# Linear attention with RMS norm and an ELU layer: the first group as four single-head-pair chains in single-bank tiles, three product buffers in the first two groups, and one norm moved behind its group's products

## The chip, the core and the metric

The kernel runs on one core of a Trainium2 chip. The core has TensorE (PE: matmuls, and PEld for its weight loads), VectorE (DVE), ScalarE (ACT), GpSimd (POOL) and SyncE (SP), each with its own instruction queue worked in order, and DMA queues that move data between the chip's memory and the core's on-chip memory SBUF. Matmul results land in PSUM, which has eight banks; one bank holds 512 fp32 columns on 128 partitions, and a tile of 1024 columns takes two. The metric is device time in microseconds. The span of a profile is counted from the first to the last instruction.

## The reference

For 8 batches and 8 heads, with 576 rows and a head dimension of 64:

```python
kv = einsum('bhsd,bhse->bhde', k, v)
out = einsum('bhsd,bhde->bhse', q, kv)
rms = sqrt(mean(out * out, axis=-1, keepdims=True) + 1e-06)
x = (out / rms * g_norm)           # then (b, s, h*d): 4608 tokens of 512
h = x @ w_in                       # 512 x 2048
g = where(h > 0, h, exp(minimum(h, 0)) - 1)
return g @ w_out                   # 2048 x 512
```

Inputs and outputs are fp32; the kernel multiplies in bf16 and sums in fp32.

## The kernel before

The 4608 tokens are worked in nine groups `T` of 512: groups 0 to 7 are the first 512 rows of each batch, group 8 is the last 64 rows of all eight. A group passes through these steps:

- **Attention.** `kv_single` multiplies k by v per head (72 small matmuls for a batch, `at["kv"]`, or two halves `kv0` and `kv1`). `se_mm` multiplies the transposed q by it, in two halves of 256 tokens (`se0`, `se1`). ACT squares (L223), DVE sums per head (L228, `sum`), ACT takes logarithm and exponential for the inverse root (L234 and L235, `inv`), DVE scales (L238, `mul`). The result is turned so that features lie on partitions, by TensorE (`x0`, `x1`, L299, emptied by ACT or DVE at L306 and L308) in groups 1 and 2, or by a transposing DMA on SP (`xd`, then `xg` on DVE) later. q is turned by TensorE in groups 0 and 1, and by a transposing DMA (`qd`, L260) after.
- **First layer.** `mm1(T, i)` for `i` of 0 to 7 makes 256 of the 2048 columns of `h`: two accumulations of four 512-column matmuls (L382), in a PSUM tile of two banks. `elu` follows: ACT takes Exp (L394); then a min and a subtraction (L403) on `eng`, which is VectorE or, in two products of group 0, GpSimd; then DVE takes the max with `h` out of PSUM (L411). With `relu`, ACT also takes a Relu of `h` (L398) and DVE adds instead, from SBUF.
- **Second layer.** `mm2(T, j, f0, f1)` sums 128 tokens `j` over 16 blocks `f` of 128 columns (L427). `mm2_quarter` does four blocks. ACT copies the result (L437) and SP stores two `j` at a time.

Nothing reorders the work: a manual schedule is set, so each engine runs its instructions in the order in which the code issues them. The framework adds semaphores where a tile is read after it is written, and where a buffer is used again.

PSUM is shared out at the start into three pools: `ps_at` (one tile of two banks, for attention), `ps_m1` (two tiles of two banks, for first-layer products) and `ps_m2` (two tiles of one bank, for second-layer sums). With `spare=True`, `mm1` puts its product into the two `ps_m2` banks.

**Group 0** has its own attention code (L495 to L614), in which features lie on partitions from the start. q comes as fp32 in two halves `s`, is cast by DVE and ACT, and turned. Then come two rounds `u`, each with two head pairs `c`: `kv_first`, `se_first`, `square_first`, `mean_first` (a matmul with a matrix of 1/64), `log_first`, `exp_first`, `scale_first`. In round 0 the two `se0` share one tile of two banks, and so do the two `mean0`. Matmuls of zeros (`idle`) stand between the steps; their results are not used. After that come sixteen first-layer matmuls (L621), by blocks `c` of features, then `mm1(0, 2)` to `mm1(0, 7)`, with the ELU step of products 3 and 5 on GpSimd, and q of batch 1 turned after product 5.

**Group 1's attention** is issued between the quarters of group 0's second layer (L649 to L671). The last quarters of `j` 2 and 3 stand after `mm1(1, 0)`, those of `j` 0 and 1 inside group 1's loop. **`group`** (L690) issues the eight products with the next group's attention (`start` gives the product after which each step stands) and with pieces of the group before's second layer (`second`). In group 1, `se0` of group 2 comes after product 5 and `se1` after product 7, both in the attention tile; the sums, the inverse root and the scaling follow one product later, and `mm2(1, 0)` and `mm2(1, 1)` stand at its end with the turnings.

POOL issues the loads of k, v, w_in, w_out and the later q, in the order of the code, between its own computing; each load waits for the landing of the eighth before it. SP loads batch 0's q and issues the stores and the transposing DMAs.

Of the kernel before, what the change touches and what calls it, by code (L numbers as in the profile page):

```python
# [16 lines left out]
def kernel(  # L17
# [36 lines left out]
    ps_at = ctx.enter_context(tc.tile_pool(name="ps_at", bufs=1, space=bass.MemoryType.PSUM))  # L54
    ps_m1 = ctx.enter_context(tc.tile_pool(name="ps_m1", bufs=2, space=bass.MemoryType.PSUM))
    ps_m2 = ctx.enter_context(tc.tile_pool(name="ps_m2", bufs=2, space=bass.MemoryType.PSUM))
# [110 lines left out]
    def kv_single(T, kv_ps, u):  # L167

        for j in range(RK):
            for l in range(2):  # L170
                for s in range(2):
                    rows = slice(s * 64, s * 64 + 64)
                    nc.tensor.matmul(  # L173
                        kv_ps[l * 64 : l * 64 + 64, s, u * 64 : u * 64 + 64],
                        lhsT=bf["k", T][rows, j, 2 * u + l, :],
                        rhs=bf["v", T][rows, j, 2 * u + l, :],
                        start=(j == 0),
                        stop=(j == RK - 1),
                    )
# [65 lines left out]
    def attention(T):  # L245
        st = {}

        def q_t():
# [5 lines left out]
            nc.scalar.copy(qT[:, 0:2, :], qt_ps[:, 0:2, :])  # L254
# [111 lines left out]
    def mm1(T, i, cols=(slice(0, 512),), relu=False, spare=False, eng=nc.vector):  # L366
# [22 lines left out]
        return elu(T, i, parts, relu, eng)  # L389

    def elu(T, i, parts, relu, eng):
# [9 lines left out]
        def rest():  # L401
            for lo, hi, h in parts:
                eng.tensor_scalar(  # L403
# [60 lines left out]
    for u in range(2):  # L464
        fetch_packed_kv("k", 0, slice(2 * u, 2 * u + 2))
        if u == 1:
            make_identity(nc, ident)
        fetch_packed_kv("v", 0, slice(2 * u, 2 * u + 2))
# [14 lines left out]
    for s in range(2):  # L483
# [11 lines left out]
    q_st = q_tile(0)  # L495
    qt_ps = [
        ps_m2.tile([P, DM], FP32, name="qt_ps", tag="mm2").bitcast(BF16).rearrange(
            "p (r t) -> p r t", r=2
        )
        for _ in range(2)  # L500
    ]
# [5 lines left out]
    idle_a = ps_m1.tile([P, 2, G], FP32, name="idle_ps", tag="mm1")  # L507
    idle(idle_a[:, 0, :], 9)
    qT0 = attp.tile([P, NPAIR, G], BF16, name="qT", tag="qT")
    for s in range(2):  # L510
        for eng, js in ((V, slice(0, 2)), (A, slice(2, 4))):
            copy_on(eng, bf["q", 0][:, js, 4 * s : 4 * s + 4, :], q_st[:, js, 4 * s : 4 * s + 4, :])
        for p in range(2):
            q_t_mm(bf["q", 0][:, :, 4 * s : 4 * s + 4, :], qt_ps[s], p)
        if s == 0:
            nc.vector.tensor_copy(out=qT0[:, 0:2, :], in_=qt_ps[0])
            idle(idle_a[:, 0, :], 2)
    nc.scalar.copy(qT0[:, 2:4, :], qt_ps[1])
    nc.tensor.matmul(
        idle_a[:, 1, 0:1],  # L520
# [5 lines left out]
    nc.vector.tensor_copy(out=g_col, in_=idle_a[:, 1, 0:1])  # L526
    idle(idle_a[:, 0, :], 6)

    kv_ps = at_tile(FP32).rearrange("p (s x) -> p s x", s=2)
# [5 lines left out]
    se0, mean0 = {}, {}  # L535

    def kv_first(u):
        kv_single(0, kv_ps, u)
        nc.vector.tensor_copy(out=kv0[:, u], in_=kv_ps[:, :, u * 64 : u * 64 + 64])

    def se_first(u):
        for l in range(2):
            ls = slice(l * 64, l * 64 + 64)
            for s in range(2):
                nc.tensor.matmul(
                    se0[2 * u + l][s * 64 : s * 64 + 64, :],
                    lhsT=kv0[ls, u, s, :],
                    rhs=qT0[ls, 2 * s + u, :],
                    start=True,
                    stop=True,  # L550
                )
# [22 lines left out]
    mean_a = ps_m1.tile([P, 2, G], FP32, name="mean_ps", tag="mm1")  # L574
    se_a = ps_m1.tile([P, 2, G], FP32, name="se_ps", tag="mm1")
    idle_b = ps_m2.tile([P, DM], FP32, name="idle_ps", tag="mm2")
    for c in range(2):
        se0[c], mean0[c] = se_a[:, c, :], mean_a[:, c, :]
    kv_first(0)
    idle(idle_b, 1)  # L580
    se_first(0)
    square_first(0, A)
    square_first(1, V)
    idle(idle_b, 3)
    mean_first(0)
    idle(idle_b, 1)
    mean_first(1)
    log_first(0)
    exp_first(0)
    log_first(1)  # L590
    kv_first(1)
    idle(idle_b, 1)
    for c in range(2, 4):
        se0[c] = ps_m2.tile([P, DM], FP32, name="se_ps", tag="mm2")
    se_first(1)
    scale_first(0)
    square_first(2, A)
    exp_first(1)
    square_first(3, V)
    scale_first(1)  # L600
    firsts = [ps_m1.tile([P, 2, G], FP32, name="h_ps", tag="mm1") for _ in range(2)]
    mean_b = at_tile(FP32).rearrange("p (c f) -> p c f", c=2)
    for c in range(2, 4):
        mean0[c] = mean_b[:, c - 2, :]
    idle(firsts[0][:, 0, :], 3)
    mean_first(2)
    log_first(2)
    exp_first(2)
    idle(firsts[0][:, 0, :], 1)
# [4 lines left out]
    scale_first(3)  # L614

    gT[0] = mlpg.tile([P, FC, G], BF16, name="gT", tag="gT")
    firsts = [ps_m1.tile([P, 2, G], FP32, name="h_ps", tag="mm1") for _ in range(2)]
    for cs in ((0, 1), (2,), (3,)):
        for f in range(4):
            for c in cs:  # L620
                nc.tensor.matmul(  # L621
                    firsts[f // 2][:, f % 2, :],
                    lhsT=w_in_sb[:, c, f * P : f * P + P],
                    rhs=x0[:, c, :],
                    start=(c == 0),
                    stop=(c == KC - 1),
                )
# [154 lines left out]
```

## Time and profile before

| | us |
|---|---|
| median of 7 runs | 301.32 (300.65 to 302.5) |
| the profiled execution | 301.71, span 299.8 |
| TensorE busy | 281.8 (94% of the span) |
| VectorE busy | 169.0 (56%) |
| ScalarE busy | 142.4 (47%) |
| GpSimd busy | 57.2 (19%) |
| granted TensorE clock, mean | 0.994 |

The stages, from the start of the span, by the timeline:

| us | stage |
|---|---|
| 1.2 to 9.9 | first loads, q of batch 0 cast and turned |
| 9.9 to 20.2 | attention of group 0 |
| 17.8 to 35.4 | first layer of group 0 |
| 35.4 to 54.4 | second layer of group 0, attention of group 1 |
| 54.4 to 84.0 | rest of group 1, attention of group 2 |
| 84.0 to 107.4 | group 2, attention of group 3 |
| 107.4 to 299.8 | groups 3 to 8 and the last store |

An average of 94% over such stages says little about any one of them. A stretch in which TensorE is full gives nothing back to a change elsewhere. In a stretch with holes, what counts is which engine's wait ends last. A row of the timeline gives the start, the length, the engine and line, what it writes and reads, and in brackets how long the engine stood idle before it and what ended that.

### The profile page before, as it was taken

The numbers are of one execution on the slowest core, as the hardware profiler recorded it, in microseconds if no ns is written. First come the engines' busy times: TensorE is split into PE (matmuls) and PEld (weight loads), VectorE is DVE, ScalarE is ACT, GpSimd is POOL, SyncE is SP. The second block draws the span as 40 slices with busy tenths as digits, with TensorE's granted clock in tenths as the row PEclk, the third lists the DMA queues.
The fourth block names the chain that finished last, engine by engine and source line by source line (L and its number), as shares of the span: only waits on it lengthen the run. The fifth ranks groups of instructions, "written<-read, shape, count | busy, mean of one in ns | idle before, by whom it ended". The sixth has DMA issues, their size and how long they took to land.

```text
span 299.8 us, 4843 instructions
## 1 busy us (share of the span) xinstructions
PE 281.8 (94%) x2017; PEld 134.7 (45%) x2017; DVE 169.0 (56%) x210; ACT 142.4 (47%) x200; POOL 57.2 (19%) x81
## 2 busy tenths in 40 slices
PE   7888789886988999999999999999999999999995
PEld 2334345443444444444444444444444444444444
DVE  5264753468238875774676467646754776544400
ACT  3378643677236545534553455444543553433311
POOL 8434925161065006000400000001100000000000
PEclk9999999999899999999999999999999999999999
DMA  8999999999999959945931505163515031101132
GB/s 197 206 205 204 140 175 193 131 220 129 187 207 170 122 132 171 176 46 129 165 110 35 128 14 108 35 149 89 149 37 140 0 108 35 70 2 70 56 84 72
DMA packets 55898, 35.97 MB, mean 120 GB/s; under 512 B 32708, under 2 KB 53444, under 8 KB 55876
## 3 DMA queue, kind: packets, MB, share of 16 engines
q0 software_dynamic: 20128, 17.30, 39.0%
q1 hardware_dynamic: 35348, 17.83, 28.5%
q10 hardware_dynamic: 400, 0.52, 0.5%
q8 instruction: 16, 0.26, 0.3%
q14 instruction: 6, 0.05, 0.0%
HBM read 36.70 MB, written 9.44 MB: 154 GB/s over the span
## 4 chain that ended last, share of the span: by engine, by line
PE 82%; ACT 5%; DVE 5%; DMA 5%; POOL 1%; issue 1%; SPq 0%; DVEq 0%; ACTq 0%; POOLq 0%
PE h_ps L382 35%; PE o_ps L427 34%; PE o_ps L741 5%; DMA qT<-q_bf 5%; ACT elu_e L394 3%; PE at L204 2%; DVE gT L411 2%; PE idle_ps L505 2%; PE at L173 1%; POOL elu_e L403 1%; PE h_ps L621 1%; DVE xs L238 1%; ACT r L564 1%; ACT elu_h L398 1%; PE at L299 1%
## 5 line engine op out<-in xcount | busy, mean ns | idle before, releaser
L382 PE MATMUL h_ps<-xT,w_in_sb 128*128 128x512 bf16 (+1 forms) x568 | 131.6, 376 | 4.4 <-DVE gT L411 3.5
L427 PE MATMUL o_ps<-w_out_sb,gT 128*128 128x512 bf16 x512 | 122.8, 383 | 0.8 <-ACT o_sb L437 0.8
L394 ACT ACTIVATE elu_e<-h_ps 128x1024 bf16<-128x1024 f32 (+1 forms) x74 | 73.8, 1003 | 92.8 <-PE h_ps L382 91.2
L411 DVE TENSOR_TENSOR gT<-elu_e,h_ps 128x1024 bf16<-128x1024 bf16 (+1 forms) x65 | 78.3, 1204 | 11.7 <-POOL elu_e L403 5.3
L382 PEld LDWEIGHTS <-w_in_sb 128*128 128x128 bf16 x568 | 54.3, 98 | 66.2 <-issue 5.4
L427 PEld LDWEIGHTS <-gT 128*128 128x128 bf16 x512 | 50.3, 99 | 61.3 <-issue 3.4
L403 DVE TENSOR_SCALAR elu_e<-elu_e 128x1024 bf16<-128x1024 bf16 x70 | 31.4, 448 | 72.1 <-ACT elu_e L394 72.0
L437 ACT COPY o_sb<-o_ps 128x512 f32<-128x512 f32 x32 | 18.8, 586 | 22.6 <-PE o_ps L427 22.6
L228 DVE TENSOR_REDUCE ss<-sq 128x16 f32<-128x1024 bf16 x16 | 19.4, 1218 | 9.7 <-ACT sq L223 9.6
L147 POOL COPY q_bf<-q_pk 128x512 bf16<-128x512 bf16 x24 | 14.7, 657 | 36.8 <-DMA q_pk<-in_q_dram 17.6
L238 DVE TENSOR_TENSOR xs<-at,ss 128x1024 bf16<-128x1024 f32 x15 | 18.3, 1217 | 0.6 <-ACT ss L235 0.6
L223 ACT ACTIVATE sq<-at 128x1024 bf16<-128x1024 f32 x15 | 15.4, 1027 | 3.3 <-PE at L204 3.3
L121 POOL DMA_DIRECT2D k_pk<-in_k_dram x10 | 7.6, 756 | 43.5 <-PE at L173 40.2
L147 POOL CAST q_bf<-st_q 128x512 bf16<-128x512 f32 x4 | 2.6, 652 | 66.2 <-DMA st_q<-in_q_dram 66.2
L741 PE MATMUL o_ps<-w_out_sb,gT 128*128 128x512 bf16 (+1 forms) x80 | 14.0, 337 | 0.0
L204 PE MATMUL at<-bd_kv,qT 128*128 128x128 bf16 x104 | 7.9, 219 | 4.5 <-DVE xs L238 3.2
L204 PEld LDWEIGHTS <-qT 128*128 128x128 bf16 x112 | 7.2, 98 | 8.2 <-issue 4.4
L741 PEld LDWEIGHTS <-gT 128*128 128x128 bf16 x80 | 7.8, 98 | 6.2
L107 POOL DMA_DIRECT2D q_pk<-in_q_dram x14 | 10.4, 752 | 0.5 <-DMA v_pk<-in_v_dram 0.5
L345 ACT CAST bd_kv<-at 64x256 bf16<-64x256 f32 x14 | 5.1, 366 | 9.7 <-PE at L173 9.6
L505 PE MATMUL idle_ps<-zeros 128*128 128x512 bf16 x23 | 8.1, 479 | 1.5 <-DVE zeros L480 1.2
L403 POOL TENSOR_SCALAR elu_e<-elu_e 128x512 bf16<-128x512 bf16 (+1 forms) x3 | 7.5, 2500 | 4.9 <-ACT elu_e L394 4.8
(64 smaller groups left out, 111.7 us busy)
## 6 DMA issues: line engine op xcount, KB each, us to landing
out_dram<-o_sb SPq DMA_DIRECT2D x16, 512.0 KB, 3.2
q_pk<-in_q_dram POOLq DMA_DIRECT2D x14, 256.0 KB, 7.6
k_pk<-in_k_dram POOLq DMA_DIRECT2D x6, 576.0 KB, 10.6
v_pk<-in_v_dram POOLq DMA_DIRECT2D x6, 576.0 KB, 12.8
w_in_sb<-in_moe_w_in_dram POOLq DMA_DIRECT2D x4, 512.0 KB, 12.6
w_out_sb<-in_moe_w_out_dram POOLq DMA_DIRECT2D x4, 512.0 KB, 7.5
k_pk<-in_k_dram POOLq DMA_DIRECT2D x4, 288.0 KB, 11.3
v_pk<-in_v_dram POOLq DMA_DIRECT2D x4, 288.0 KB, 10.4
```

Of the source, the lines that this page charges most:

```text
L147: eng.tensor_copy(out=out_, in_=in_)
L204: nc.tensor.matmul(ov[:, u, :, s, :], lhsT=qT(p, j), rhs=bd_kv[:, T, p, :], start=True, stop=True,)
L223: nc.scalar.activation(sq, se_ps, AF.Square)
L228: nc.vector.reduce_sum(out=ss, in_=sq.rearrange("p c (h e) -> p (c h) e", h=H), axis=AX.X)
L238: nc.vector.tensor_tensor(out=xs.rearrange("p c (h e) -> p (c h) e", h=H), in0=se_ps.rearrange("p c (h e) -> p (c h) e", h=H), in1=ss.to_b ...
L382: nc.tensor.matmul(h_ps[a][:, cs], lhsT=w_in_sb[:, c, f * P : f * P + P], rhs=x(c, cs), start=(c == 0), stop=(c == KC - 1),)
L394: nc.scalar.activation(e[:, lo:hi, :], ps, AF.Exp)
L403: eng.tensor_scalar(out=e[:, lo:hi, :], in0=e[:, lo:hi, :], scalar1=1.0, scalar2=1.0, op0=ALU.min, op1=ALU.subtract,)
L411: nc.vector.tensor_tensor(out=gT[T][:, 2 * i + lo : 2 * i + hi, :], in0=e[:, lo:hi, :], in1=h, op=ALU.add if relu else ALU.max,)
L427: nc.tensor.matmul(o_ps[T, j], lhsT=gT[T][:, f, j * P : j * P + P], rhs=w_out_sb[:, f, :], start=(f == 0), stop=(f == FC - 1),)
L437: nc.scalar.copy(o_sb[T][:, j % 2, :], o_ps.pop((T, j)))
L741: nc.tensor.matmul(ps, lhsT=gT[B][:, f, j * P : j * P + P], rhs=w_out_sb[:, f, cols], start=(f == 0), stop=(f == FC - 1),)
```

## The change

- k and v of batch 0 are loaded head pair by head pair, in eight transfers.
- Group 0's attention uses a pool `ps_head` of its own, over all eight banks: two for kv, six single ones. The three later pools are opened when it closes, with `reuse_waits="tile"`, so that a tile waits for the readers of the banks that it takes over.
- The rounds become four steps `c`, one head pair each. The casts and copies of q are shared out otherwise between DVE and ACT, and there are 23 idle matmuls where there were 27.
- The first two products of group 0 lie in a `ps_m1` tile and in the attention tile. Products 3 and 6 of group 0, and 2 and 5 of group 1, go into the `ps_m2` banks. All ELU steps are on VectorE. Relu is used in products 0, 4 and 7 of group 0 and 1 and 4 of group 1.
- One of the two copies of group 1's transposed q goes from ACT to DVE.
- All quarters of group 0's second layer are done before group 1's first product, in the order of `j` 2, 3, 0, 1. That product is no longer cut into column halves.
- Group 1 is written out: `se0` of group 2 after product 6, `se1` after all products and half of `mm2(1, 0)`, in a `ps_m1` tile of its own; then the sums and scalings, 24 second-layer matmuls, and the turnings with a quarter of `mm2(1, 2)` after each. The rest of `mm2(1, 2)` and `mm2(1, 3)` stands beside products 1 to 6 of group 2.

```diff
-    def kv_single(T, kv_ps, u):
+    def kv_single(T, kv_ps, u, ls=(0, 1)):
...
-            for l in range(2):
+            for l in ls:
...
-            nc.scalar.copy(qT[:, 0:2, :], qt_ps[:, 0:2, :])
+            nc.vector.tensor_copy(out=qT[:, 0:2, :], in_=qt_ps[:, 0:2, :])
             nc.scalar.copy(qT[:, 2:4, :], qt_ps[:, 2:4, :])
...
-    for u in range(2):
-        fetch_packed_kv("k", 0, slice(2 * u, 2 * u + 2))
-        if u == 1:
+    for c in range(4):
+        fetch_packed_kv("k", 0, slice(c, c + 1))
+        if c == 2:
             make_identity(nc, ident)
-        fetch_packed_kv("v", 0, slice(2 * u, 2 * u + 2))
+        fetch_packed_kv("v", 0, slice(c, c + 1))
...
+    kv_ps = ps_head.tile([P, 2, G], FP32, name="kv_ps", tag="kv")
+    se0 = {c: bank(c) for c in range(2)}
+    idle_ps, g_ps = bank(2), bank(3)
...
-    for s in range(2):
-        for eng, js in ((V, slice(0, 2)), (A, slice(2, 4))):
...
+    for s, eng in ((0, A), (1, V)):
+        for js in (slice(0, 2), slice(2, 4)):
+            copy_on(
+                V if (s, js.start) == (0, 0) else eng,
...
+        copy_on(eng, qT0[:, 2 * s : 2 * s + 2, :], qt_ps[s])
         if s == 0:
...
-    idle(idle_a[:, 0, :], 6)
+    idle(idle_ps, 1)
...
+    kv_first(0)
+    idle(idle_ps, 1)
+    se_first(0)
+    square_first(0, A)
...
+    for c in range(2):
+        mean0[c] = bank(2 + c)
+    kv_first(1)
+    mean_first(0)
+    log_first(0)
+    idle(idle_ps, 1)
+    se_first(1)
+    square_first(1, A)
+    exp_first(0)
+    idle(idle_ps, 2)
+    kv_first(2)
+    mean_first(1)
+    log_first(1)
+    scale_first(0)
...
+    head.close()
+    ps_at = ctx.enter_context(tc.tile_pool(name="ps_at", bufs=1, space=bass.MemoryType.PSUM, reuse_waits="tile"))
...
-    elu(0, 0, [(0, 2, firsts[0])], True, V)()
-    elu(0, 1, [(0, 2, firsts[1])], False, V)()
+    for i in range(2):
+        elu(0, i, [(0, 2, firsts[i])], i == 0)()
     for i in range(2, 8):
-        mm1(0, i, relu=i in (2, 4, 6), spare=i in (2, 5), eng=Q if i in (3, 5) else V)()
+        mm1(0, i, relu=i in (4, 7), spare=i in (3, 6))()
...
-    for j in range(J):
+    order = (2, 3, 0, 1)
+    for j in order:
         mm2_quarter(0, j, 0)
...
-    rest = mm1(1, 0, (slice(0, 256), slice(256, 512)))
-    for j in (2, 3):
+    for j in order:
         mm2_quarter(0, j, 3)
-    rest()
...
-    second = {2: [(0, 0, 12, 16)], 3: [(0, 1, 12, 16)]}
-    group(1, at, {"kv": 2, "se0": 5, "se1": 7}, second, (1, 3, 5, 7), 1)
+    for i in range(8):
+        rest = mm1(1, i, relu=i in (1, 4), spare=i in (2, 5))
+        rest()
+        if i == 3:
+            at["kv"]()
+        if i == 6:
+            at["se0"]()
+    mm2(1, 0, 0, 8)
+    at["se1"](ps_m1.tile([P, 2, G], FP32, name="se_ps", tag="mm1"))
+    for n in range(2):
+        at[f"sum{n}"]()
+        at[f"inv{n}"]()
+    at["mul0"]()
+    at["mul1"]()
+    mm2(1, 0, 8, FC)
+    mm2(1, 1, 0, FC)
+    at["x0"]()
+    mm2_quarter(1, 2, 0)
+    at["x1"]()
+    mm2_quarter(1, 2, 1)
...
-            second = {i: [(1, 2 + i // 4, 4 * (i % 4), 4 * (i % 4) + 4)] for i in range(8)}
+            quarters = [(1, 2 + i // 4, 4 * (i % 4), 4 * (i % 4) + 4) for i in range(2, 8)]
+            second = {i + 1: [piece] for i, piece in enumerate(quarters)}
```

## The prediction

> **What bounds it now.** I read the page's shares first, then the table of stretches, the list of TensorE's waits, and last the timeline of the first 110 us. In the shares PE leads; the stretches (length, then busy time of each engine, granted clock, DMA share, GB/s) say where it is not full:
>
> ```profile
> PE 281.8 (94%) x2017; PEld 134.7 (45%) x2017; DVE 169.0 (56%) x210; ACT 142.4 (47%) x200; POOL 57.2 (19%) x81
> ```
> ```profile
> 110.00:280.00 170.00, 169.52 (x1131) 79.50 (x1130) 105.27 (x124) 77.60 (x108) 11.74 (x18) 1.00 0.44 90
> ...
> 70.00:74.00 4.00, 1.69 (x15) 0.93 (x13) 3.76 (x5) 2.80 (x5) 0.00 (x0) 1.00 1.48 117
> 74.00:78.00 4.00, 4.00 (x13) 1.50 (x11) 2.49 (x3) 1.16 (x3) 0.00 (x0) 0.57 1.47 122
> ```
>
> From 110 to 280 us PE is full (169.5 of 170) and the change leaves that code alone, so all that can move lies before group 3's first product at 107.43. At 70 to 74 us PE works 1.69 of 4 us, and then it runs at a clock of 0.57. TensorE's waits in that first part (total, times, longest):
>
> ```profile
> PE h_ps L382 <- DVE gT L411: 3.5, 4, 1.6
> PE at L204 <- DVE xs L238: 3.2, 2, 2.3
> ```
>
> A product waits until VectorE has emptied a PSUM buffer, and group 2's second attention product until the first one's scaling is done. The timeline (start, length, what, idle before) dates them:
>
> ```profile
> 13.34 0.38 PE L561 MATMUL mean_ps<-sq,means 128*128 128x512 bf16 x1 [0.86 <-DVE sq L558]
> 13.76 0.69 ACT L564 ACTIVATE r<-mean_ps,eps_col 128x512 f32<-128x512 f32 x1 [1.91 <-PE mean_ps L561]
> 19.41 0.75 DVE L570 SCALAR_TENSOR_TENSOR xT<-se_ps,g_col,r 128x512 bf16<-128x512 f32 x1 [0.49 <-ACT r L567]
> 20.96 1.02 ACT L394 ACTIVATE elu_e<-h_ps 128x1024 bf16<-128x1024 f32 x1 [1.59 <-PE h_ps L621]
> ...
> 26.89 3.64 POOL L403 TENSOR_SCALAR elu_e<-elu_e 128x1024 bf16<-128x1024 bf16 x1 [4.82 <-ACT elu_e L394]
> 31.84 3.61 PE L382 MATMUL h_ps<-xT,w_in_sb 128*128 128x512 bf16 x16 [1.55 <-DVE gT L411]
> ...
> 72.97 0.61 PE L204 MATMUL at<-bd_kv,qT 128*128 128x128 bf16 x8 [2.31 <-DVE xs L238]
> 73.42 5.30 PE L427 MATMUL o_ps<-w_out_sb,gT 128*128 128x512 bf16 x16
> 83.98 1.89 PE L382 MATMUL h_ps<-xT,w_in_sb 128*128 128x512 bf16 x8 [0.91 <-DVE xT L308]
> ```
>
> The first mean is done at 12.27, but its logarithm starts at 13.76, after the second mean: both lie in one tile. POOL's ELU step takes 3.64 us, and PE stands 1.55 behind it. The sixteen matmuls at 73.42 take 5.30 us; the next sixteen, at 79.00, take 3.62: the slow clock costs 1.7.
>
> **The sum, stage by stage.** I follow each engine in program order, with these durations: eight 512-column matmuls 1.73; ACT Exp or Relu over 1024 columns 1.02, the next starting 0.92 after it, over 512 0.55; DVE min 0.43, max out of PSUM 1.22 (512 columns: 0.69), add after a Relu 0.69; square 0.60; log then exponential 0.71; kv copy 0.29; scaling 0.75. Between engines: kv copy to product 0.05, product to square 0.46, mean to log 0.42, last scaling to ELU 0.80. All are read off the timeline.
>
> *Head.* DVE casts q's second half twice (6.10 to 7.1) and copies its transpose (7.65 to 8.34) where ACT did; ACT takes the first half's copy (1.01 against DVE's 0.69, still done at 7.14). Idle matmuls here go from six to one, and they no longer wait for g. So the first kv product moves from 9.89 to 8.3, its copy (behind g's on DVE) to 8.75, the first square from 11.24 to 9.55. Then, pair by pair: mean 10.2, log 10.62; second square 11.2; exponential 11.75; second mean 11.85; third product 12.5, square 12.96; fourth product 13.55; DVE copies and squares it 14.0 to 15.4; fourth mean 15.46, log 15.88, exponential 16.59, scaling 17.26 to 18.0; ELU 18.8 against 20.96: **2.15 us gained**. That the pools close behind this costs nothing: in the built order each new tile waits for the last reader of its own banks, the latest being the second scaling (16.1), and the third and fourth have other banks.
>
> The loads: batch 0's k and v become eight transfers of 144 KB instead of four of 288. That is four more issues of 0.75 on POOL, and w_in is issued from 7.8 instead of 4.79, each part also behind one of the first four pieces (landed by about 9). The queue is still fed, as k and v end only at 11.9, so I cost it at nothing; without that cover, each us it stands dry delays all later weights by one.
>
> *Group 0.* DVE gets three ELU steps back from POOL (7.5 us there, 3 x 0.43 here), one Relu fewer (+0.53 on DVE, -0.92 on ACT), and half of the qT copy (0.69). Against that PE has a third place for products (in 3 and 6 of 0 to 7, and the first pair uses the attention tile). Products 2 to 4 run unbroken from 19.05 to 24.25; product 5 waits for DVE's third max, 25.07 (0.85 lost); transposes 26.85 to 27.93; 6 and 7 to 31.4. The two halves of the qT copy are now in line: ACT's waits for DVE's, which stands behind the fifth max (29.8), so it runs 30.5 to 31.55 and delays Exp 6 behind it. Only k.v of batch 1 (31.55) and two quarter products (max 6 done at 34.0) meet that, and the order 2, 3, 0, 1 puts others before them. Second kv half 35.45; attention products 36.8 (40.69 before, the same 1.35 after); first turning 42.85; the last four quarters 45.65 to 50.1, with the same wait for the o_sb copy inside (0.8). Before, an equal amount of work was done at 54.45: **4.35 gained so far**.
>
> *Group 1.* PE's work from there is 25.7 us: eight products 13.84, kv 0.78, two attention products 1.22, 40 second-layer matmuls 8.63, two turnings 1.22. Each product finds its place empty: product 3 needs max 0 by 55.3, done 54.8; 5 needs max 2 by 59.55, done 58.35; 6 needs max 3 by 61.3, done 60.1. The second attention product has a tile of its own and needs max 6 (66.1) at 67.1, not the first one's scaling: the 2.31 goes. What is late next is DVE: max 7, two sums and two scalings in a row, 67.2 to 73.0, beside 24 matmuls; the first turning (72.9) finds its scaling done (71.85). Only four matmuls now part the turnings, so the second waits for ACT to empty the first (74.85): 0.55 lost. Group 2 begins at 76.45. Before it began at 83.98 with 1.73 less done, so 85.7: **9.25 gained so far**.
>
> *Group 2.* Its first and last products have no second-layer piece beside them, and DVE needs 1.65 a product and 2.44 a norm half. The second attention product still waits for the scaling (88.05; 0.7 against 0.86), and group 3's first product, with 2.6 us behind product 6's matmuls, waits for its max and the last g scaling (99.05; 0.85 against 0.34). Group 3 starts at 99.05 against 107.43. **Sum: -8.4 us.** The profiled execution took 301.71 (span 299.8 and 1.9 around it), so 293.3; it lies 0.4 over the median of the seven.
>
> **Loads now come near.** They run at about 190 to 205 GB/s written, and land (POOL waits for them):
>
> ```profile
> 10.47 0.70 POOL L121 DMA_DIRECT2D k_pk<-in_k_dram  x1 [0.70 <-DMA k_pk<-in_k_dram]
> 11.89 0.71 POOL L121 DMA_DIRECT2D v_pk<-in_v_dram  x1 [0.72 <-DMA v_pk<-in_v_dram]
> 14.44 0.76 POOL L139 DMA_DIRECT2D w_out_sb<-in_moe_w_out_dram  x1 [1.84 <-DMA w_in_sb<-in_moe_w_in_dram]
> ```
>
> Adding bytes at that rate (an estimate): w_out's first part at 31 (needed 32.0), k and v of batch 1 at 34 (35.45), w_out's second part at 36.7 (37.65), third 39.3 (41.3). The slack is 1 us. In its favour, POOL no longer holds w_out's second part until 30.50; the DMA share sank to 0.80 at 34 to 38 us because of it.
>
> **Two rules weighed.** The Trainium skill, "DMA: Bandwidth & Descriptors", section on the anatomy of one DMA, prices each transfer at about 2.0 us fixed plus its bytes, and its rules ask for 1 MiB at least; that speaks against the split. Row: 288 KB landed 1.42 us apart, 512 KB of w_in about 2.6, both near 5 us per MB, so no fixed share shows when transfers queue. By the row the split costs 0; by the rule four more cost 8.0 us. I take the row, and keep the rule as the end of a rival. The other: "TensorE: Matmul & The Clock Gate", part 1, halves the clock after an idle window of about 3.4 us. Here a gap of 2.31 came before the slow matmuls (5.30 against 3.62). By the row, the slow spell goes with the gap; by the rule it would have another cause and stay, 1.7 us: 295.0. I take the row; the longest gap in my sum is 0.9.
>
> **Costs the trace does not show.** A 512-column min on DVE lies between 0.22 and 0.43; I take 0.25, and eight at 0.43 would put 1.4 on DVE, partly beside PE: 0 to +1. A 64-row kv copy: 0.29 as for 128 rows, at least 0.15; four on the chain, 0 to -0.5. The head's 23 idle matmuls instead of 27 might let the clock fall there: 0 to +1.7. Waiting on single banks in place of pool-wide: 0 to -0.5.
>
> **Rivals.** (1) As summed, 293.3, with its own bounds 291.8 to 294.8: 0.55. (2) The load stream binds: if it is 3.5 us later than my estimate, w_out's second part lands at 40.2 against 37.65 and shifts all that follows by 2.5: 295.8. For it, the slack of 1 us and a DMA share already above 1.1; against it, the dry stretch that goes. 0.17. (3) The slow clock stays or comes elsewhere, or VectorE's longer list in groups 0 and 1 costs one more wait of 1.5: 295.0 to 296.5. For it, DVE's last sums end within 1 us of need in three places. 0.17. (4) Slower: the fixed price per transfer is paid in the queue. 8.0 us later, w_out's second part lands at 44.7, so PE stands 7.0 us in all, once in the head for its last k and v and again in group 0, and loses 1.7 to the clock after each stand as at 73.42: 303.7. It decides from a delay of 6 us on (293.3 + 5 beyond the slack + 3.4). Against it, landings in proportion to bytes. 0.05. (5) The rest, 0.06, is a gain beyond (1), to 291.
>
> The range 291.3 to 297.3 leaves out (4), the end of (2) and little else. About 0.3%, or 0.9 us, is what a measurement can tell from no change; 0.92 faster, 0.03 within, 0.05 slower.
>
> **What would show it.** ELU's first Exp near 18.8; product 5 waiting for a max near 25; attention products near 36.8; no slice with a clock under 0.9 after the start; group 2's first product near 76.5, group 3's near 99. Wrong if w_out or batch 1's k ends PE's wait, if a granted clock near 0.57 stands anywhere, or if VectorE's max ends waits of over 1 us in group 1.

## The result, and the profile after

The changed kernel takes 296.74 us, median of 12 executions (294.27 to 301.14), against 301.04 before (31 executions, 300.51 to 302.5). The ratio is 0.9827, with a 95% interval of 0.9804 to 0.985. So it is faster, by 1.7%, which is clear of the noise, and the median lies in the range of the prediction. But the forecast was 293.3, a gain of 8.4 us, and the medians differ by 4.3, about half of that. One thing has to be known to read the numbers below: a ratio leaves out the executions that count as slow, which for the changed kernel are those above 300 us, with all three profiled ones of it (here and in the repeats `again` and `again_b`) among them, while medians and ranges hold every execution; the changed kernel's spread over 7 us, those of before over 2.

The profiled execution of after is the slowest of its twelve (301.14, span 299.4). First the shares and the table of stretches (length, then busy time of each engine, granted clock, DMA share, GB/s):

```profile
PE 282.8 (94%) x2005; PEld 134.4 (45%) x2005; DVE 171.9 (57%) x221; ACT 139.1 (46%) x197; POOL 51.8 (17%) x82
```
```profile
110.00:280.00 170.00, 169.61 (x1132) 79.60 (x1130) 105.43 (x124) 77.27 (x107) 11.95 (x18) 1.00 0.40 86
70.00:74.00 4.00, 4.00 (x25) 1.99 (x24) 4.00 (x4) 1.66 (x6) 0.00 (x0) 1.00 1.42 104
...
98.00:102.00 4.00, 0.85 (x4) 0.20 (x2) 1.55 (x3) 1.02 (x1) 0.00 (x0) 1.00 1.75 126
102.00:106.00 4.00, 0.83 (x3) 0.29 (x4) 1.76 (x4) 0.00 (x0) 0.00 (x0) 0.53 1.16 258
106.00:110.00 4.00, 4.00 (x13) 1.59 (x12) 0.91 (x2) 1.02 (x1) 0.00 (x0) 0.62 0.32 72
```

The late stretch is full as before. The hole at 70 to 74 us is gone (4.00 of 4), and the slow clock that followed it too. But there is a new hole: from 98 to 106 us PE works 1.7 of 8 us, and then its clock is 0.53 and 0.62. TensorE's waits up to 112 us (total, times, longest) name it:

```profile
PE h_ps L379 <- DVE xT L324: 6.3, 1, 6.3
...
PE at L201 <- DVE xs L235: 0.8, 1, 0.8
PE h_ps L379 <- DVE gT L408: 0.8, 1, 0.8
```

The wait for a PSUM place has shrunk from 3.5 us to 0.8, the one for the scaling from 3.2 to 0.8. One wait of 6.3 stands in their place: a product that needs group 3's transposed x. The timeline (start, length, what, idle before) dates it:

```profile
19.89 1.02 ACT L391 ACTIVATE elu_e<-h_ps 128x1024 bf16<-128x1024 f32 x1 [1.69 <-PE h_ps L635]
...
26.24 1.89 PE L379 MATMUL h_ps<-xT,w_in_sb 128*128 128x512 bf16 x8 [0.78 <-DVE gT L408]
...
77.03 1.89 PE L379 MATMUL h_ps<-xT,w_in_sb 128*128 128x512 bf16 x8
...
83.76 1.48 POOL L104 DMA_DIRECT2D q_pk<-in_q_dram  x2
...
85.96 0.77 POOL L118 DMA_DIRECT2D v_pk<-in_v_dram  x1
...
88.76 7.85 SPq L317 DMA_TRANSPOSE xT<-xs  x2
...
100.34 0.49 DVE L324 TENSOR_SCALAR xT<-xT,g_col 128x1024 bf16<-128x1024 bf16 x1 [3.63 <-DMA xT<-xs]
...
104.62 0.48 DVE L324 TENSOR_SCALAR xT<-xT,g_col 128x1024 bf16<-128x1024 bf16 x1 [2.13 <-DMA xT<-xs]
...
105.17 3.60 PE L379 MATMUL h_ps<-xT,w_in_sb 128*128 128x512 bf16 x8 [6.32 <-DVE xT L324]
```

Group 2 begins at 77.03 (forecast 76.45). Its successor should have begun at 99.05 and begins at 105.17: DVE's scalings wait for the transposing DMAs (issued at 88.76 and 95.09), which land only at 100.3 and 104.6, and PE waits for DVE. Its first eight matmuls then take 3.60 where eight take 1.89 at full clock. In the profile of before the rows of the loads, of the transposing DMAs and of the first scaling read:

```profile
84.12 1.48 POOL L107 DMA_DIRECT2D q_pk<-in_q_dram  x2
...
88.49 0.75 POOL L121 DMA_DIRECT2D v_pk<-in_v_dram  x1
...
96.63 7.55 SPq L320 DMA_TRANSPOSE xT<-xs  x2
...
104.50 0.48 DVE L327 TENSOR_SCALAR xT<-xT,g_col 128x1024 bf16<-128x1024 bf16 x1
```

There the DVE row has no bracket: the x was there when DVE came to it. Batch 5's loads (two of q, then k, then v) start at the same time in both profiles (84.12, 83.76), but the transposing DMA has moved forward by 7.9. It used to come 12.5 us behind the first of the four loads and 8.1 behind the last; now it comes 5.0 and 2.8 behind.

### The profile page after: what moved, and what is told of

Its sections match the earlier page's. It is cut to its first block, busy times and chain, and to the rows that moved or that the text cites. A ratio compares the mean times of both kernels' runs of the same rounds, so it can differ in the third digit from the quotient of the medians.

```text
span 299.4 us, 4836 instructions
## 1 busy us (share of the span) xinstructions
PE 282.8 (94%) x2005; PEld 134.4 (45%) x2005; DVE 171.9 (57%) x221; ACT 139.1 (46%) x197; POOL 51.8 (17%) x82
## 4 chain that ended last, share of the span: by engine, by line
PE 77%; DMA 10%; DVE 7%; ACT 4%; issue 1%; SPq 0%; DVEq 0%
PE h_ps L379 33%; PE o_ps L424 32%; PE o_ps L769 5%; DMA qT<-q_bf 5%; DVE gT L408 3%; DMA xT<-xs 3%; DMA st_q<-in_q_dram 2%; PE at L201 2%; ACT elu_e L391 1%; DVE elu_e L400 1%; PE at L170 1%; ACT o_sb L434 1%; DVE xs L235 1%; PE bank L502 1%; ACT elu_h L395 1%
## 5 line engine op out<-in xcount | busy, mean ns | idle before, releaser
L379 PE MATMUL h_ps<-xT,w_in_sb 128*128 128x512 bf16 x560 | 132.8, 383 | 7.1 <-DVE xT L324 6.3
L424 PE MATMUL o_ps<-w_out_sb,gT 128*128 128x512 bf16 x512 | 121.0, 380 | 0.7 <-ACT o_sb L434 0.7
L391 ACT ACTIVATE elu_e<-h_ps 128x1024 bf16<-128x1024 f32 (+1 forms) x75 | 72.8, 981 | 96.2 <-PE h_ps L379 94.5
L408 DVE TENSOR_TENSOR gT<-elu_e,h_ps 128x1024 bf16<-128x1024 bf16 (+1 forms) x70 | 81.2, 1160 | 7.3
L400 DVE TENSOR_SCALAR elu_e<-elu_e 128x1024 bf16<-128x1024 bf16 (+1 forms) x76 | 33.2, 437 | 73.9 <-ACT elu_e L391 73.9
L235 DVE TENSOR_TENSOR xs<-at,ss 128x1024 bf16<-128x1024 f32 x14 | 17.0, 1217 | 0.0
L118 POOL DMA_DIRECT2D k_pk<-in_k_dram x12 | 8.3, 695 | 45.8 <-PE at L170 40.0
L220 ACT ACTIVATE sq<-at 128x1024 bf16<-128x1024 f32 x14 | 14.4, 1026 | 2.7 <-PE at L201 2.7
L104 POOL DMA_DIRECT2D q_pk<-in_q_dram x14 | 10.5, 757 | 1.1 <-DMA v_pk<-in_v_dram 0.7
L502 PE MATMUL bank<-zeros 128*128 128x512 bf16 x23 | 8.9, 497 | 1.2 <-DVE zeros L477 1.2
L324 DVE TENSOR_SCALAR xT<-xT,g_col 128x1024 bf16<-128x1024 bf16 x12 | 5.8, 480 | 5.8 <-DMA xT<-xs 5.8
```

Of the source, the lines that this page charges most:

```text
L220: nc.scalar.activation(sq, se_ps, AF.Square)
L235: nc.vector.tensor_tensor(out=xs.rearrange("p c (h e) -> p (c h) e", h=H), in0=se_ps.rearrange("p c (h e) -> p (c h) e", h=H), in1=ss.to_b ...
L379: nc.tensor.matmul(h_ps[a][:, cs], lhsT=w_in_sb[:, c, f * P : f * P + P], rhs=x(c, cs), start=(c == 0), stop=(c == KC - 1),)
L391: nc.scalar.activation(e[:, lo:hi, :], ps, AF.Exp)
L400: nc.vector.tensor_scalar(out=e[:, lo:hi, :], in0=e[:, lo:hi, :], scalar1=1.0, scalar2=1.0, op0=ALU.min, op1=ALU.subtract,)
L408: nc.vector.tensor_tensor(out=gT[T][:, 2 * i + lo : 2 * i + hi, :], in0=e[:, lo:hi, :], in1=h, op=ALU.add if relu else ALU.max,)
```

## Experiments

The theories, in the order in which they came up. **A**: group 3's two transposing DMAs are late because batch 5's loads are then in the same DMA engines. **B**: something in groups 0 to 2 varies from one execution to the next. **C**: in some executions the head has too few matmuls, the clock is halved there, and about 3 us are lost. **D**: the low clock at 102 to 110 us is only what follows group 3's wait. **E**: the eight quick transfers of k and v delay the second half of q.

### The change repeated, the loads held back, the DMA taken away

`again` is the changed kernel once more, with no edit. `gate_x` holds batch 5's loads until group 3's x is there, by a one-column copy on GpSimd ahead of them; `turn_pe` has TensorE turn group 3's x, so no transposing DMA is left there.

```diff
+            if T == 3:
+                gate = const.tile([P, 1], BF16, name="gate")
+                nc.gpsimd.tensor_copy(out=gate, in_=xT[3](3, slice(0, 512))[:, 3, 127:128])
             fetch(T + 2)
```
```diff
             start = {"kv": 0, "se0": 1, "xd0": 2, "se1": 3, "xd1": 4, "xg0": 5, "xg1": 6}
+            if T == 2:
+                start = {"kv": 0, "se0": 1, "se1": 3, "x0": 5, "x1": 6}
```

Expected of `again`:

> The changed kernel once more, to see an execution nearer to the median than the one profiled (301.14). Theory A (the two transposing DMAs of group 3's x share the DMA engines with the loads of batch 5, issued at 83.8 to 86): group 3's first product waits again for the last g scaling, by 1 to 3 us where the total is near 295, against 6.3 at 301, and everything before it stands where it stood within 0.3 us. Theory B (something in groups 0 to 2 varies, such as the clock or the first loads): the first product of group 2 moves by 2 us or more from 77.0.

Expected of `gate_x`:

> One GpSimd copy of one column, which reads group 3's scaled x, stands before the loads of batch 5, so that these are issued after group 3's x has landed. Theory A: both transposing DMAs land within 3 to 4 us, group 3's first product starts at 99 to 100, the slow clock behind it goes, and the time is 292 to 294 with a spread under 2 us. Theory B, or the transposing DMAs being slow by themselves behind the stores on their own queue: no change, 295 to 297.

Expected of `turn_pe`:

> Group 3's x is turned by TensorE (after products 5 and 6 of group 2) in place of the two transposing DMAs. It adds 1.2 us of matmuls and one ACT pass of 1.1. Both explanations that put the loss into the transposing DMAs: the wait before group 3's first product is under 1.5 us, time 293 to 295. Theory B: 296 to 298, the added work on top.

Measured, on one chip: `again` 298.06 (294.9 to 300.35, ratio 0.9867, 0.9825 to 0.9908), `gate_x` 295.51 (293.01 to 297.34, 0.9818, 0.9779 to 0.9856), `turn_pe` 296.01 (295.21 to 298.28, 0.9843, 0.9808 to 0.9879). The intervals overlap, so these times alone separate nothing, and both variants missed the times expected under A (292 to 294 with a spread under 2 us, and 293 to 295). The traces say more. `again` has the wait for xT again, 4.74 us. In `gate_x` it is 0.71:

```profile
88.49 7.56 SPq L317 DMA_TRANSPOSE xT<-xs  x2
...
96.36 0.48 DVE L324 TENSOR_SCALAR xT<-xT,g_col 128x1024 bf16<-128x1024 bf16 x1
...
99.29 1.90 PE L379 MATMUL h_ps<-xT,w_in_sb 128*128 128x512 bf16 x8 [0.71 <-DVE xT L324]
```

The DMAs go out at the same time as in after (88.49), DVE waits for nothing, and PE begins at 99.29 where the forecast said 99.05, at full clock. This execution took 293.01, 8.13 less than the profiled one of after: 5.88 by the earlier start, 1.90 by the clock up to the second product (it starts at 103.55 here, at 111.33 there), 0.35 elsewhere. A and D fit these two traces. B falls as the main cause: up to 77 us the two agree within 0.3. This profile does not yet prove A, though: its GpSimd was ahead, with the cast before these loads done by 80.5 (83.8 in after), so that even without the gate the loads would have gone out 8 us before the transposing DMA (an estimate) and not 5. The profile of `gate_b` below has no such head start.

But `gate_x` had three executions of 296.5 to 297.3, at a clock of 0.988, and three of 293.0 to 294.6. The profiled execution of `turn_pe` (298.1, clock 0.988) shows where such a clock can come from. Its stretches:

```profile
8.00:12.00 4.00, 3.66 (x33) 1.66 (x32) 1.43 (x4) 0.42 (x1) 4.00 (x7) 0.64 1.21 203
12.00:16.00 4.00, 3.64 (x43) 1.39 (x42) 0.29 (x1) 1.98 (x4) 2.03 (x3) 0.50 1.24 206
```

The head runs at half clock here, and the first ELU begins at 23.43 instead of about 20. That is C, seen once. It comes after PE waited 1.11 us for the second half of q. The other executions near a clock of 0.988 were not profiled.

### Four variants: more idle matmuls, k and v in four transfers, the copies of q

To test C and E, and one edit costed at nothing. `idle_more` is the changed kernel with 6 idle matmuls for 2 after the first half of q, and 2 for 1 after g. `gate_idle` has the gate and these. `gate_kv4` has the gate, and k and v of batch 0 in four transfers as before. `gate_qt` has the gate, and both copies of group 1's transposed q on ACT as before.

```diff
         if s == 0:
-            idle(idle_ps, 2)
+            idle(idle_ps, 6)
...
-    idle(idle_ps, 1)
+    idle(idle_ps, 2)
```
```diff
-    for c in range(4):
-        fetch_packed_kv("k", 0, slice(c, c + 1))
...
+    for u in range(2):
+        fetch_packed_kv("k", 0, slice(2 * u, 2 * u + 2))
```
```diff
-            nc.vector.tensor_copy(out=qT[:, 0:2, :], in_=qt_ps[:, 0:2, :])
+            nc.scalar.copy(qT[:, 0:2, :], qt_ps[:, 0:2, :])
```

Expected of `idle_more`:

> The changed kernel with five idle matmuls more in the head (six instead of two before q's second half is turned, two instead of one after g). Theory C (beside the late transposing DMAs, in some executions the head has too few matmuls, its clock falls to half, and 3 us go): no execution has a mean clock near 0.988 with the head's ELU after 22; the spread that stays is that of group 3's wait, 294 to 298.5. Rival D (the low clock comes from group 3's wait alone): clocks and times as in the changed kernel, median 296 to 298, and the five matmuls add up to 0.5.

Expected of `gate_idle`:

> The late loads of batch 5 and the five idle matmuls together. Theory A with C: every execution has a clock of 0.998 or more and takes 292.8 to 294.8, median 293.8. D: as with the late loads alone, 293 to 297.3 in two clusters 3 us apart.

Expected of `gate_kv4`:

> The late loads of batch 5, and batch 0's k and v in four transfers of 288 KB as before. Theory E (eight quickly issued transfers delay q's second half, which landed at 6.75 to 7.34 with eight and at 6.10 with four): q's second half lands at 6.1 to 6.3, the first kv product waits for v instead, at about 9.0, and the first Exp of ELU moves by less than 0.5 from 20.1; low clocks in the head become rarer, since PE's gap before the second half shrinks. Rival (the split costs nothing and gives the early start): q lands at 6.75 or later all the same and the head is 0.4 to 1 us longer.

Expected of `gate_qt`:

> The late loads of batch 5, and both copies of group 1's transposed q on ACT as before. By the prediction's step the two copies in line cost almost nothing, because quarter products cover them: time within 0.5 us of the late loads alone at equal clock. Rival (they delay k.v of batch 1 and all after it): k.v of batch 1 starts about 1 us earlier than 32.6 and the time falls by 0.7 to 1.2.

| on one chip | median | range | ratio, interval |
|---|---|---|---|
| `idle_more` | 293.84 | 293.69 to 294.61 | 0.9756, 0.9736 to 0.9776 |
| `gate_idle` | 294.39 | 293.81 to 295.78 | 0.9778, 0.9754 to 0.9802 |
| `gate_kv4` | 294.16 | 293.55 to 295.61 | 0.9774, 0.975 to 0.9797 |
| `gate_qt` | 293.96 | 293.39 to 296.51 | 0.9775, 0.9744 to 0.9807 |

`gate_idle` was expected within 292.8 to 294.8; three of its six executions are above that, up to 295.78. E holds for the landing of q. In `gate_kv4` (timeline, the head):

```profile
6.01 0.82 DVE L144 CAST q_bf<-st_q 128x512 bf16<-128x512 f32 x2 [0.90 <-DMA st_q<-in_q_dram]
...
8.95 0.47 PE L170 MATMUL kv_ps<-v_pk,k_pk 64*64 64x64 bf16 x18 [0.92 <-DMA v_pk<-in_v_dram]
```

The cast of q's second half starts at 6.01; with eight transfers it starts at 6.75 to 7.34. But then the first kv product waits 0.92 for v, and the ELU begins at 20.20, as with eight (19.89 to 20.20 where the clock was full and the idle matmuls are the same). The split delays q and brings k and v earlier, and the two cancel on the path. `gate_qt` begins kv of batch 1 at 32.66, 12.75 us after its first ELU; after begins it at 32.67, 12.78 after: the copies cost nothing where they stand.

The surprise is `idle_more`. Without the gate, its x lands in time: group 3 begins at 99.84 with a wait of 0.71. Idle matmuls in the head should not bear on a DMA 80 us later. Either it was the chip, or something else had changed.

### On one chip: the change, more idle matmuls, the gate; and two places for products

The first three again, as `again_b`, `idle_b` (which is `idle_more`) and `gate_b` (which is `gate_x`), on one chip; with them `two_bufs`, which is `idle_more` with the third place for products taken away in groups 0 and 1:

```diff
-        mm1(0, i, relu=i in (4, 7), spare=i in (3, 6))()
+        mm1(0, i, relu=i in (4, 7))()
...
-        rest = mm1(1, i, relu=i in (1, 4), spare=i in (2, 5))
+        rest = mm1(1, i, relu=i in (1, 4))
```

Expected of `again_b`:

> The changed kernel unchanged, beside its variants on one chip. Theory A (group 3's two transposing DMAs are late when batch 5's loads are issued just before them) with C (clock halved in the head of some executions): a mixture, best runs 294 to 295 at a clock of 0.998 or more, others 297 to 301 at 0.98 to 0.99, median 296 to 298.5. Rival (the five even runs with more idle matmuls came from the chip they ran on, not from the idle matmuls): all runs here 294 to 295.2 at a clock of 0.997 or more.

Expected of `idle_b`:

> The variant with 6 and 2 idle matmuls in place of 2 and 1, nothing else. Theory C: no run under a clock of 0.995, 293.7 to 294.6, at least 2 us under the unchanged kernel's median on the same chip. Theory A says that the late transposing DMA can still come here: if it does, single runs at 297 to 298. Rival (chip): within 0.7 us of the unchanged kernel's median, whatever that is.

Expected of `gate_b`:

> Batch 5's loads held behind group 3's transposed x, idle matmuls as in the change. Theories A and C: two clusters, 293.0 to 294.6 at a clock of 0.998 or more and 296.4 to 297.4 at 0.988, and no run above 298, where the unchanged kernel has some. Rival (the late DMA is not from those loads): the unchanged kernel's spread, up to 301.

Expected of `two_bufs`:

> The variant with more idle matmuls, and the third place for products taken away again in groups 0 and 1 (their products then alternate between two places, as before the change). If the third place is what lets products run on (prediction, groups 0 and 1): each product from the fourth on waits about 0.9 us for the max of the one two before it (exponential 1.02, min 0.43 and max 1.22 against a product of 1.73), six to eight such waits of max on gT in the first 70 us, 4 to 7 us in all: 298 to 301. Rival (VectorE's 1.65 us a product is the bound anyway, the third place only moves the wait): within 1 us of the same variant with three places.

| on one chip | median | range | ratio, interval |
|---|---|---|---|
| `again_b` | 301.0 | 294.4 to 303.58 | 0.9776, 0.9744 to 0.9809 |
| `idle_b` | 293.92 | 293.54 to 297.61 | 0.9773, 0.9734 to 0.9812 |
| `gate_b` | 295.81 | 294.64 to 298.9 | 0.9831, 0.9793 to 0.9869 |
| `two_bufs` | 303.18 | 300.87 to 305.38 | 1.0064, 1.004 to 1.0088 |

It is not the chip: here the unchanged kernel has four of six executions above 300, and `idle_b` none. (Its best two, 294.4 and 294.72, are level with `idle_b`, which is why the two ratios agree.) Its median was expected at 296 to 298.5 and came at 301.0; `idle_b` has one execution at 297.61, which C did not allow. `gate_b` missed its expectation of two clusters, and one execution was above 298.

The profiles of `again_b` and `gate_b` are the test of A, since they agree up to here: the cast that stands before batch 5's loads begins at 83.33 and 83.39, and x goes out at 90.56 and 90.35. In `again_b` the loads go out at 85.55:

```profile
90.56 7.95 SPq L317 DMA_TRANSPOSE xT<-xs  x2
...
106.08 3.60 PE L379 MATMUL h_ps<-xT,w_in_sb 128*128 128x512 bf16 x8 [5.26 <-DVE xT L324]
```

In `gate_b` they are held until 101.38:

```profile
90.35 7.55 SPq L317 DMA_TRANSPOSE xT<-xs  x2
...
101.14 1.90 PE L379 MATMUL h_ps<-xT,w_in_sb 128*128 128x512 bf16 x8 [0.71 <-DVE xT L324]
```

From issue to landing x's two DMAs take 9.6 us in the first and 3.7 in the second (medians of the two). With the loads gone the wait and the slow clock behind it go too: A and D hold. The rival that x is late behind the stores of its own queue falls, since these are the same in both.

`two_bufs` loses 9.3 us against `idle_b`; 4 to 7 were expected. TensorE's waits up to 115 us:

```profile
PE h_ps L379 <- DVE gT L408: 5.5, 5, 2.8
PE o_ps L424 <- DVE gT L408: 2.1, 1, 2.1
```

Group 1 begins at 57.49 instead of 51.69 and group 2 at 86.71 instead of 77.49, so within this schedule the third place is worth 5.8 us in group 0 and 3.4 in group 1. That is not what the change won by it: before had a third place in group 0 already, for products 2 and 5, so `two_bufs` has fewer places there than before, not as many, as its expectation says. The expectation put each wait at 0.9; the longest is 2.8, and it left out that the second layer's first sum waits too. These rows make 7.6 of TensorE's waiting, of which `idle_b` has 0.9 as well. Another 1.7 is the clock: behind the wait of 2.1, 16 second-layer matmuls take 5.30 us where they take 3.63 in `idle_b`, at a granted clock of 0.66 and then 0.50. These make 8.4 of the 9.3. The rival, within 1 us, falls.

### What the idle matmuls had changed

The traces of after and of `idle_b` differ from 46.6 us on. In after, where POOL has just cast batch 2's q:

```profile
46.50 1.48 POOL L104 DMA_DIRECT2D q_pk<-in_q_dram  x2
46.58 4.54 SPq L257 DMA_TRANSPOSE qT<-q_bf  x1
...
61.69 3.06 POOL L144 COPY q_bf<-q_pk 128x512 bf16<-128x512 bf16 x4 [12.22 <-ACT elu_e L391]
```

and in `idle_b`:

```profile
46.60 3.28 SPq L257 DMA_TRANSPOSE qT<-q_bf  x1
46.87 1.48 POOL L104 DMA_DIRECT2D q_pk<-in_q_dram  x2 [0.30 <-POOL q_bf L144]
...
58.87 2.53 POOL L144 COPY q_bf<-q_pk 128x512 bf16<-128x512 bf16 x4 [9.04 <-DMA q_pk<-in_q_dram]
```

Both DMAs become free with the cast. In after, batch 3's loads go out 0.08 us before the transposing DMA of batch 2's q; in `idle_b` they wait 0.30 for the cast and go out 0.27 after it. The two kernels differ only in the idle matmuls of the head, and `gate_kv4`, with another edit in the head, has the order of `idle_b` too; what in the built programs turns it is not shown. Sorted by this order, the profiles fall in two groups; only `gate_x`, the first of the first row's range, reaches into the second:

| first at 46.6 us | kernels | batch 3's q cast at |
|---|---|---|
| the loads | after, `again`, `again_b`, `gate_x`, `gate_b`, `gate_qt`, `turn_pe` | 59.4 to 64.6 |
| the transposing DMA | `idle_more`, `idle_b`, `gate_idle`, `gate_kv4`, `two_bufs` | 58.0 to 60.0 |

POOL works in order, and its loads of a batch stand behind the cast of the batch before, so a late cast moves the later loads. (It is not all that moves them: in `idle_b` batch 4's cast comes 5.7 us earlier than in `idle_more`, with the same order.) What counts then is how long before group 3's transposing DMA batch 5's loads go out:

| | first q load | v load, the last | x's DMA | lead of the first, of the last | x from issue to landing | PE's wait for x |
|---|---|---|---|---|---|---|
| after | 83.76 | 85.96 | 88.76 | 5.0, 2.8 | 10.5 | 6.32 |
| `again_b` | 85.55 | 87.74 | 90.56 | 5.0, 2.8 | 9.6 | 5.26 |
| `again` | 82.89 | 85.09 | 88.70 | 5.8, 3.6 | 9.4 | 4.74 |
| `idle_more` | 80.26 | 82.45 | 89.04 | 8.8, 6.6 | 4.3 | 0.71 |
| `idle_b` | 74.53 | 81.19 | 89.03 | 14.5, 7.8 | 3.8 | 0.71 |
| before | 84.12 | 88.49 | 96.63 | 12.5, 8.1 | 4.5 | 0.34 |
| `two_bufs` | 73.85 | 90.41 | 98.48 | 24.6, 8.1 | 3.7 | 0.71 |

A batch is two loads of 256 KB and two of 576 KB; at the 200 GB/s of these stretches that is about 8.5 us (an estimate). In before, `idle_b` and `two_bufs` k and v, the larger part, went out long after q, so the lead of the last load is the better guide: x is late at 2.8 to 3.6 and in time from 6.6 on; nothing on record lies between. A transposing DMA of q meets the loads in the same way in `gate_b`, `gate_qt` and `again_b`: it lands 17 to 19 us after its issue, and PE waits 1.6 us for batch 3's in `gate_b`, 1.4 for batch 2's and 1.0 for batch 3's in `gate_qt`, 1.7 for batch 3's in `again_b`.

The test, as theory **F**: the changed kernel with nothing but a one-column copy on GpSimd between cast and loads, so that the loads go out after the transposing DMA. The idle matmuls stay as in the change.

```diff
+    nudge = const.tile([P, 1], BF16, name="nudge")
+    nc.gpsimd.tensor_copy(out=nudge, in_=bf["q", 2][:, J - 1, H - 1, D - 1 : D])
     fetch(3)
```

> The changed kernel with one GpSimd copy of a single column between its cast of batch 2's q and the loads of batch 3, so that the loads are issued about 0.2 us later, after SyncE's transposing DMA of that q instead of 0.08 us before it; idle matmuls as in the change (2 and 1). Theory F (this order decides: in all profiles where the transposing DMA went first, at 46.6 to 46.8 us, it landed 11 to 12 us later and batch 4's q was cast at 58.9 to 60.0; where the two loads went first it took 13 to 18 and the cast came at 59.4 to 64.6, which makes batch 5's loads collide with group 3's x): cast of batch 4's q by 60, batch 5's loads issued by 81, group 3's first product at 99 to 100.5, median 293.5 to 295, no run over 298. Theory C (idle matmuls in the head decide): as the changed kernel, several runs of 297 to 301 at a clock of 0.98 to 0.99, median 296 to 301. Both: the late x gone, but single runs at 296.4 to 297.4 and 0.988.

(What this calls the cast of batch 4's q is that of batch 3's.) Measured on a chip of its own, where before took 301.2: 294.63, range 294.06 to 295.18, ratio 0.9779, 0.9753 to 0.9805. The timeline:

```profile
46.56 3.20 SPq L257 DMA_TRANSPOSE qT<-q_bf  x1
46.59 0.19 POOL L725 COPY nudge<-q_bf 128x1 bf16<-128x1 bf16 x1
47.08 1.48 POOL L104 DMA_DIRECT2D q_pk<-in_q_dram  x2 [0.30 <-issue]
...
57.40 3.04 POOL L144 COPY q_bf<-q_pk 128x512 bf16<-128x512 bf16 x4 [7.35 <-ACT elu_e L391]
...
80.54 1.62 POOL L104 DMA_DIRECT2D q_pk<-in_q_dram  x2
...
89.96 7.56 SPq L317 DMA_TRANSPOSE xT<-xs  x2
...
100.75 1.90 PE L379 MATMUL h_ps<-xT,w_in_sb 128*128 128x512 bf16 x8 [0.71 <-DVE xT L324]
```

The loads go out 0.52 us after the transposing DMA instead of 0.08 before, that DMA lands in 10.2 us (15.4 in after), the cast comes 4.3 us earlier than in after, the leads are 9.4 and 7.1, and x is in time. Group 3 begins 0.25 later than F allowed, behind a slower head; the rest came as expected. No execution passes 295.2, where the changed kernel without an edit had 14 of 23 above 297 over its three sets. F holds so far as one profile and five executions show it. The median is 2 to 6 us lower than in the three sets; in the ratios the difference is 0.5%, 0.9% and nothing, so what is won is mainly that the late executions stay away. Two things are not separated: the order, and the loads going out 0.5 us later as such. And the order is not the only thing that counts, since `gate_x` has an early cast with the loads first. C is seen once more here, and is not the main cause; the stretch of `nudge` in the head:

```profile
8.00:12.00 4.00, 3.64 (x41) 1.76 (x40) 1.04 (x3) 0.60 (x1) 4.00 (x7) 0.60 1.21 203
```

The clock falls, the ELU begins at 21.45, and group 3 at 100.75 against 99.82 in `idle_b`; yet this execution took 294.36. Whether the additional idle matmuls prevent it is not settled: four profiles with them (`idle_more`, `idle_b`, `gate_idle`, `two_bufs`) do not show it, two of nine with fewer do.

The best version found is the changed kernel with the transposing DMA first, as `idle_more`: 0.9756 (0.9736 to 0.9776), and 0.9773 when it was repeated as `idle_b`. `gate_kv4` (0.9774), `gate_qt` (0.9775) and `nudge` (0.9779) cannot be told from it.

## Why the prediction was right, and where it failed

**Step by step.** Starts in us, the forecast beside the profile of after:

| | forecast | after |
|---|---|---|
| cast of q's second half | 6.10 | 6.75 |
| first kv product | 8.3 | 8.64 |
| first ELU | 18.8 | 19.89 |
| product 5 of group 0 | 25.07 | 26.24 |
| kv of batch 1 | 31.55 | 32.67 |
| attention products of group 1 | 36.8 | 37.98 |
| group 1 | 50.1 | 50.96 |
| group 2 | 76.45 | 77.03 |
| group 3 | 99.05 | 105.17 |

- **Head: right in kind, 1.1 us short.** The cast of q's second half starts 0.65 late, of which 0.34 is left at the first kv product. The sum kept q at 6.10 and asked of the split only what it does to the weights: "The queue is still fed, as k and v end only at 11.9, so I cost it at nothing". But the eight transfers are issued faster (0.55 us each on POOL, not the 0.75 of the sum; 0.74 before), and q lands later. From there the delay grows pair by pair, to 0.95 at the third pair's product and 1.09 at the ELU; why was not traced. `gate_kv4` shows that the split as such neither gains nor loses at the ELU.
- **Group 0: right.** Product 5 waits for a max as forecast (0.78 against 0.85); from the ELU to kv of batch 1 it is 12.78 against 12.75. The wait that the third place was to remove is real, as `two_bufs` shows.
- **Group 1: right, a little better.** 26.07 us to group 2 against 26.35. The second attention product no longer waits for a scaling; the second turning waits 0.38 for ACT (0.55 forecast; the sum's own terms add up to 0.1 less than its 76.45). The hole of 2.31 and its slow clock went together.
- **Group 3's first product failed.** The step: "group 3's first product, with 2.6 us behind product 6's matmuls, waits for its max and the last g scaling (99.05; 0.85 against 0.34)". It took the scaling's input as given. The transposing DMAs were moved forward with group 2, and the sum followed the step on PE, ACT and DVE, but not its DMAs past batch 5's loads. With the loads out of the way the step holds: from group 2 to group 3 it is 22.3 us in `gate_x`, `idle_b` and `nudge`, 22.6 in the forecast, with a wait of 0.71. In the profile of after it cost 6.1 us, and 1.9 more by the clock.
- **The clock.** "By the row, the slow spell goes with the gap" was right. But "the longest gap in my sum is 0.9" fell with the late x, and so did "no slice with a clock under 0.9 after the start": the prediction's own sign of being wrong, a clock near 0.57, stands in the profile of after, 0.53 and 0.62 behind group 3's wait. The head's clock, put at 0 to +1.7, cost about 3.4 at the ELU in `turn_pe` and 1.6 in `nudge`.
- **Loads.** They did come near, but not where the sum looked: no w_out or k and v of batch 1 ended a long wait. Rival 2, "The load stream binds", had the loads right and the place wrong; rival 4, the fixed price per transfer, did not come. Rival 3, "The slow clock stays or comes elsewhere", names what followed the late x, but not its cause.

So the rest of the sum holds: six variants in whose profile x is in time (`idle_more`, `idle_b`, `gate_idle`, `gate_kv4`, `gate_qt`, `nudge`) have medians of 293.8 to 294.6 against the forecast of 293.3. `gate_x` and `gate_b` stay at 295.5 and 295.8, with the low clock of some executions and the late q. The three profiles of the changed kernel without an edit all have the late x. Its executions of 297 to 298 were not profiled, so how many of them owe their time to it is not shown. That the median of 296.74 lies in the range is in part luck: it is the middle of a mixture, 7 of the 12 executions lie in the range, and the medians of both repeats (298.06 and 301.0) lie outside it.

## What to carry to other kernels

When work moves forward in time, its DMAs move with it and may now meet transfers that used to be done; list for each moved transfer which other transfers are then under way, and how much lead these have against the time that their bytes need. Two DMAs freed by the same event on two queues have an order that nobody wrote down; an edit elsewhere can turn it, so an experiment that seems to work for its own reason should be compared with the control in the order of issue too. A cheap instruction on the loads' engine can fix the order: the one-column copy took 0.19 us.

## What was not expected of the hardware

- At 46.6 us the order of two DMAs, turned from 0.08 us one way to 0.3 or 0.5 the other, goes with how long the transposing DMA of q takes: 10 to 12 us to land in the six profiles where it went first, 13 to 18 in the seven where the loads went first. The loads themselves land later too when they go first (k in 17 to 23 us against 13 to 16). At 60.3 us in `two_bufs` the q loads go first as well, but k and v 7 us later, and the transposing DMA lands in 11.5; in the other profiles, with k and v close behind, it takes 16 to 19 at this step. So it is not the order alone. What in the DMA engines makes this so was not tried.
- A late x leads to a second loss, since the clock falls behind the wait: 8 matmuls in 3.60 us after 6.32 us of waiting.
- The head's clock fell after gaps of 1.1 us in `turn_pe` and `nudge`, and did not after the same gap in `gate_b`. In `two_bufs` it fell after a gap of 2.06 us and not after one of 2.79. The Trainium skill, "TensorE: Matmul & The Clock Gate", part 1, speaks of an idle window of about 3.4 us that runs freely, so that the same kernel differs from run to run; the difference between executions agrees with it, the length of the gap alone does not tell.
